# Attention and gated FFN on one core: q and k loaded in whole rows, outputs stored in 32-row pieces, masks taken off GpSimd

## The chip, the core and the metric

The kernel runs on one core of a Trainium2 chip. The metric is the device time of one execution, in microseconds (us). The kernel before took 558.26 us (median of three runs, 554.87 to 558.68). The profiled execution took 555.26 us, and its span from the first to the last recorded instruction is 553.5 us; times of single operations below are from that execution.

## The reference

Eight batches of eight heads, 576 positions, head size 64. Scores below the row's maximum less tau are cut, the rest goes through a softmax; the heads of a position make one row of 512, which is normalised by its root mean square and goes through a gated FFN with 1536 hidden values.

```python
scores = scale * np.matmul(q, k.transpose(0, 1, 3, 2))
thresh = np.max(scores, axis=-1, keepdims=True) - tau
scores = np.where(scores >= thresh, scores, -1000000000.0)
attn = softmax(scores)
x = np.matmul(attn, v)             # -> (4608, 512)
xn = x / rms(x) * rms_g
out = (silu(xn @ w_gate) * (xn @ w_val)) @ w_out
```

## The kernel before

**Tiles and stages.** The work is cut in 144 steps. One step takes a pair of heads and 128 query rows: 32 chunks of the first 512 positions of a batch ("m"), and 4 chunks that put the last 64 positions of two batches together ("v"), four head pairs each. A step goes through these operations:

- TensorE writes scores of both heads into PSUM (`s_ps`, L684).
- VectorE moves them to SBUF negated and scaled and takes the running minimum in the same instruction (`ssb`, `mx`, L717).
- GpSimd adds tau to that minimum (`nth`, L758).
- The threshold and the exponential. The list `WAYS` gives the way of a step from its number modulo 3, from step 16 (`FIRST`) on. The way "pp" is two activations on ScalarE that cut (L769) and one exponential of both heads (L776). The way "pg" does head 0 in that manner (L769, L773), and head 1 with an exponential on ScalarE (L788), a mask on GpSimd (L802) and their product on GpSimd (L807). Every third step is "pg", 42 in all.
- The fp16 weights `wsb` are transposed to `wt`, on TensorE for the first 16 steps (L821), and after that by a DMA transpose that SyncE issues (L836).
- TensorE multiplies by v for two steps at a time (AV, L854 and L859), and VectorE divides by the sum (L876, L878, L883).

After four steps a chunk is complete. It is squared (L900), scaled (L903 to L908) and transposed by DMA (`xnT`, L912). Groups of four chunks (the first two groups have two) go through the FFN: gate (L966), tanh (L980), value (L971), products on VectorE (L983, L988), output product (L1037, L1012 for the last group), eviction (L1050, L1052) and the store (L1058 for "m" chunks, L1062 for "v").

**Inputs.** Batches 0 and 1 come in natural rows and are transposed by TensorE. From batch 2 on (`BLOCKED`), `emit_block_loads` brings q and k so that VectorE can transpose them in blocks of 32 x 32 (L384, L389, L394). SBUF partition 64h + 32e + s gets, of the heads 4h to 4h + 3, half e of the head size, so a run in memory is 32 floats or 128 bytes. A batch takes eight such loads of 288 KB (L370). k is split as position = 18s + r, and q as position = 32r + s, so the 128 rows of an output chunk of these batches are consecutive rows, and one store writes them.

**Order.** Nothing of the order is left to the queues. Each operation is recorded with its engine, an assumed cost (`COST`, `DMA_NS`), a priority and its dependences; `order_ops` plays the program through with these costs, adds the offsets of `RANK` to the priorities, and writes out one fixed order for each engine. All loads, stores and DMA transposes are issued by SyncE in that one order, except for two late stores and one load on ScalarE and the output weights on GpSimd. [...] The second batch ahead is loaded while a batch is computed; a block load waits until the VectorE transposes of the block data before have read the buffer `qkx`.

Of the kernel before, what the change touches and what calls it, by code (L numbers as in the profile page):

```python
# [21 lines left out]
)  # L22
DMA_NS = dict(qkb=1900.0, qk=1250.0, tl=700.0, v=880.0, vt=350.0, wt=1700.0, xt=800.0, out=800.0, w=820.0, wo=2500.0)
SWITCH = 125.0

RANK = dict(
    ACT={"emit_ffn/ev": 260, "emit_ffn/store": 60, "emit_ffn/tanh": -350, "emit_k_tail/ev": -140, "emit_q_tail/ev": -100, "emit_qk/ev": 280,
        "emit_softmax/ex": 18, "emit_softmax/ex2": -350, "emit_softmax/prelu": 18, "emit_x/sq": -320},
    DVE={"emit_av/half": -10.4, "emit_blocks/turn_k": 30, "emit_blocks/turn_kt": 20, "emit_blocks/turn_q": 50, "emit_burst/ttr": -14.1, "emit_ffn/ev":
        140, "emit_ffn/gate": -80, "emit_ffn/silu": -13.4, "emit_k_tail/ev": -130, "emit_qk/ev": -100, "emit_softmax/ev": 410},  # L30
    PE={"emit_av/fn": -260, "emit_burst/fn": -160, "emit_ffn/gmm": 18.5, "emit_ffn/omm": 22, "emit_k_tail/tr": 250, "emit_q_tail/tr": -200,
        "emit_qk/tr": 170, "emit_softmax/tr": -190},
    POOL={"emit_softmax/mask": 110, "emit_softmax/nthr": -180, "emit_softmax/take": -170, "emit_x/mean": -60, "emit_x/norm": -41, "round_/<lambda>":
        -47.8, "main/<lambda>": 670, "main/cast": -260},
)
# [114 lines left out]
def kernel(  # L150
# [12 lines left out]
    nc = tc.nc  # L163
# [28 lines left out]
    LEAD = TAIL // 32  # L192
    qkx = sb("qkx", [128, 2 * S * NP])
    kx = qkx[:, 0:S * NP].rearrange("p (r a d) -> p r a d", a=NP, d=32)
    qx = qkx[:, S * NP:2 * S * NP].rearrange("p (a r d) -> p a r d", a=NP, d=32)
    qkn = [qkx[:, 1024 * i:1024 * (i + 1)].rearrange("p (j c h d) -> p j c h d", j=2, c=4, d=D) for i in range(NQK)]
# [159 lines left out]

    assert BLOCKED == 2 and S * NP < 1024 * NQK
    turned = []

    def emit_block_loads(b, prio):  # L360

        los = {}
        for j, src in ((1, k), (0, q)):
            before = turned[j] if turned else [x for t in tr_of for x in t[-NQK:]] + ([] if j else tail_load["use", 0])
            for h in range(2):
                for e in range(2):
                    def load(o, j=j, src=src, h=h, e=e):
                        rows = slice(64 * h + 32 * e, 64 * h + 32 * e + 32)
                        heads = src[b, NP * h:NP * h + NP, :, 32 * e:32 * e + 32]
                        nc.sync.dma_start(out=kx[rows] if j else qx[rows], in_=heads.rearrange("a (s r) d -> s r a d", r=RUN)  # L370
                                          if j else heads.rearrange("a (r s) d -> s a r d", r=RUN))

                    pr = prio + BLOCK_STEP * len([x for y in los.values() for x in y])
                    los.setdefault(j, []).append(gated(add("SP", COST["sp_qb"], pr, before, load, dma=DMA_NS["qkb"], bulk=True), pr))
                    los[j][-1].lat = LAT_QB
        turned[:] = [[], []]
        return los

    def emit_blocks(b, p, prio, los):
# [242 lines left out]
    def emit_batch_inputs(b):  # L622
# [318 lines left out]
    clock = [0.0]  # L941

    def emit_ffn(slot, parts, ready_step, pace, streamed):

# [80 lines left out]
        for j, (ci, _) in enumerate(parts):  # L1025
# [158 lines left out]
LAG = 8.0  # L1184
LAT_TR = 2000.0
LAT_LD = 2000.0
# [73 lines left out]
```

## Time and profile before

| what | value |
|---|---|
| span of the profiled execution | 553.5 us |
| TensorE busy | 527.7 us, 95% |
| VectorE busy | 467.7 us, 85% |
| ScalarE busy | 427.7 us, 77% |
| GpSimd busy | 255.9 us, 46% |
| DMA packets, bytes | 325,318, 89.03 MB |
| packets under 512 bytes | 307,840 |
| HBM read, written | 37.75 MB, 9.44 MB |
| last score product starts its burst | 490.2 us |

A matmul's end is modelled in the profile, so a TensorE that is called busy may still stand for part of that time. From some 50 us on, the attention of later chunks and the FFN of earlier ones share TensorE. After the last scores at 492 us there is only the FFN of the last groups left, in which TensorE is unbroken up to 548 us, and the last stores end at 553 us. The groups of instructions which the change touches are, in the page's columns (line, engine, operation, out and in, count, busy us, mean ns, idle time before them and its releaser):

```profile
L769 ACT ACTIVATE ssb<-ssb,nth 128x576 f32<-128x576 f32 x246 | 181.1, 765 | 35.5 <-POOL nth L758 35.2
L776 ACT ACTIVATE wsb<-ssb 128x1152 f16<-128x1152 f32 x102 | 118.2, 1159 | 3.4 <-DMA wt<-wsb 1.8
L802 POOL TENSOR_SCALAR wsb<-ssb,nth 128x576 f16<-128x576 f32 x42 | 72.5, 1726 | 37.6 <-DMA wt<-wsb 34.1
L807 POOL TENSOR_TENSOR wsb<-wsb,esb 128x576 f16<-128x576 f16 x42 | 53.7, 1279 | 4.0 <-ACT esb L788 0.7
L788 ACT ACTIVATE esb<-ssb,nth 128x576 f16<-128x576 f32 x42 | 32.3, 768 | 13.8 <-POOL nth L758 13.8
```

And the DMAs that it touches, in the list of DMA issues (out and in, queue, operation, count, KB each, median us from issue to landing):

```profile
out_dram<-osb SPq DMA_DIRECT2D x29, 256.0 KB, 2.9
qkx<-in_k_dram SPq DMA_DIRECT2D x24, 288.0 KB, 5.0
qkx<-in_q_dram SPq DMA_DIRECT2D x24, 288.0 KB, 5.2
wt<-wsb SPq DMA_TRANSPOSE x128, 3.9
```

### The profile page before, as it was taken

To read this page: it belongs to the slowest core of one execution; us is meant where nothing else is said; L and a number is where in the kernel's file an instruction comes from. 1 tells how busy PE (TensorE), PEld (TensorE's weight loads), DVE (VectorE), ACT (ScalarE), POOL (GpSimd) and SP (SyncE) were. 2 spreads that over 40 slices of the span, in tenths; PEclk is the share of its full clock that TensorE was granted. 3 is DMA by queue.
4 is the path that set the end of the run, shared out by engine and by line. 5 is a ranking of instruction groups with operands and counts; after the bars stand their busy time and mean duration, and the time that the engine had idled before them with its cause. 6 is when DMAs were issued, how large, how long until landed. Compare 5 with 4: busy or idle time off the path is not lost.

```text
span 553.5 us, 14260 instructions
## 1 busy us (share of the span) xinstructions
PE 527.7 (95%) x5336; PEld 276.9 (50%) x5336; DVE 467.7 (85%) x1342; ACT 427.7 (77%) x648; POOL 255.9 (46%) x418
## 2 busy tenths in 40 slices
PE   8999979997989999999999999999899999999996
PEld 4666646654545445544444545444454444445442
DVE  4898969986999899979998999899879997995661
ACT  5999978878888889778977898679857999893220
POOL 2378643384454654445455544365444653542000
PEclk9999999998999999999999999999989999999999
DMA  8999999999999899999999799999999767764102
GB/s 201 221 288 290 172 147 149 188 184 163 160 157 179 177 136 161 170 180 208 154 162 215 162 145 150 176 202 168 149 182 204 132 101 120 123 105 100 59 0 97
DMA packets 325318, 89.03 MB, mean 161 GB/s; under 512 B 307840, under 2 KB 317568, under 8 KB 325248
## 3 DMA queue, kind: packets, MB, share of 16 engines
q1 hardware_dynamic: 322320, 85.76, 90.1%
q0 software_dynamic: 1600, 1.57, 2.0%
q8 instruction: 42, 0.69, 0.6%
q10 hardware_dynamic: 1328, 0.79, 0.5%
q14 instruction: 28, 0.23, 0.2%
HBM read 37.75 MB, written 9.44 MB: 85 GB/s over the span
## 4 chain that ended last, share of the span: by engine, by line
PE 54%; DMA 18%; ACT 9%; DVE 8%; issue 5%; POOL 4%; SPq 1%; DVEq 0%; POOLq 0%; ACTq 0%
PE s_ps L684 16%; DMA wt<-wsb 11%; PE ring L966 10%; PE ring L971 10%; PE ring L1037 9%; DVE ssb L717 4%; ACT ssb L769 4%; PE ring L859 3%; ACT wsb L776 3%; DMA stg<-in_moe_w_val_dram 3%; DMA xnT<-xn 2%; PE s_ps L1012 2%; ACT th L980 1%; PE ring L854 1%; DVE sl L983 1%
## 5 line engine op out<-in xcount | busy, mean ns | idle before, releaser
L769 ACT ACTIVATE ssb<-ssb,nth 128x576 f32<-128x576 f32 x246 | 181.1, 765 | 35.5 <-POOL nth L758 35.2
L717 DVE CUSTOM_DVE_ANT_0 ssb<-s_ps,zrow 128x576 f32<-128x576 f32 (+8 forms) x288 | 171.5, 636 | 9.8 <-PE s_ps L684 7.6
L684 PE MATMUL s_ps<-qkt 64*64 64x288 f32 (+9 forms) x2240 | 173.8, 418 | 4.4 <-DVE mxp L717 3.4
L776 ACT ACTIVATE wsb<-ssb 128x1152 f16<-128x1152 f32 x102 | 118.2, 1159 | 3.4 <-DMA wt<-wsb 1.8
L684 PEld LDWEIGHTS s_ps<-qkt 64*64 64x64 f32 (+1 forms) x2240 | 82.6, 136 | 70.1 <-issue 28.7
L966 PE MATMUL ring<-xnT,wg 128*128 128x512 f16 (+1 forms) x464 | 109.7, 359 | 4.1 <-DMA xnT<-xn 4.1
L971 PE MATMUL ring<-xnT,wv 128*128 128x512 f16 (+1 forms) x464 | 109.8, 360 | 0.4 <-DVE hf L988 0.4
L758 POOL TENSOR_SCALAR nth<-mx 128x2 f32<-128x2 f32 x144 | 31.5, 219 | 149.4 <-DVE mx L717 140.9
L802 POOL TENSOR_SCALAR wsb<-ssb,nth 128x576 f16<-128x576 f32 x42 | 72.5, 1726 | 37.6 <-DMA wt<-wsb 34.1
L980 ACT ACTIVATE th<-ring 128x512 f32<-128x512 f32 (+1 forms) x116 | 62.8, 542 | 32.4 <-PE ring L966 32.1
L983 DVE SCALAR_TENSOR_TENSOR sl<-th,ring 128x512 f32<-128x512 f32 (+1 forms) x116 | 72.4, 626 | 13.6 <-ACT th L980 13.0
L966 PEld LDWEIGHTS <-wg 128*128 128x128 f16 x480 | 43.8, 98 | 53.6 <-issue 10.8
L971 PEld LDWEIGHTS <-wv 128*128 128x128 f16 x480 | 43.6, 98 | 53.9 <-issue 16.3
L717 DVE CUSTOM_DVE_ANT_0 ssb<-s_ps,zrow,mxp 128x128 f32<-128x128 f32 (+7 forms) x112 | 53.3, 512 | 20.0 <-PE s_ps L684 19.4
L807 POOL TENSOR_TENSOR wsb<-wsb,esb 128x576 f16<-128x576 f16 x42 | 53.7, 1279 | 4.0 <-ACT esb L788 0.7
L859 PE MATMUL ring<-va,wt 128*128 128x65 f16 (+1 forms) x1264 | 52.4, 194 | 0.0
L1037 PE MATMUL ring<-wo,hf 128*128 128x512 f16 x216 | 50.0, 381 | 0.0
L859 PEld LDWEIGHTS <-wt 128*128 128x128 f16 (+1 forms) x1280 | 47.2, 100 | 4.8
L788 ACT ACTIVATE esb<-ssb,nth 128x576 f16<-128x576 f32 x42 | 32.3, 768 | 13.8 <-POOL nth L758 13.8
L854 PE MATMUL ring<-va,wt 128*128 128x130 f16 (+1 forms) x158 | 32.0, 226 | 8.0 <-DMA wt<-wsb 7.8
L988 DVE TENSOR_TENSOR hf<-ring,sl 128x512 f16<-128x512 f32 (+1 forms) x59 | 37.1, 628 | 2.1 <-PE ring L971 0.3
L988 DVE TENSOR_TENSOR stg<-ring,sl 128x512 f16<-128x512 f32 (+1 forms) x57 | 35.7, 627 | 3.0 <-PE ring L971 0.4
(76 smaller groups left out, 494.9 us busy)
## 6 DMA issues: line engine op xcount, KB each, us to landing
vst<-in_v_dram SPq DMA_DIRECT2D x32, 256.0 KB, 4.3
out_dram<-osb SPq DMA_DIRECT2D x29, 256.0 KB, 2.9
qkx<-in_k_dram SPq DMA_DIRECT2D x24, 288.0 KB, 5.0
qkx<-in_q_dram SPq DMA_DIRECT2D x24, 288.0 KB, 5.2
stg<-in_moe_w_gate_dram SPq DMA_DIRECT2D x6, 512.0 KB, 5.8
stg<-in_moe_w_val_dram SPq DMA_DIRECT2D x6, 512.0 KB, 6.8
wt<-wsb SPq DMA_TRANSPOSE x128, 3.9
qkx<-in_k_dram SPq DMA_DIRECT2D x7, 256.0 KB, 5.2
```

The source lines that it names most:

```text
L684: nc.tensor.matmul(s_ps[h][rows, at:at + hi - lo], lhs(hs), k_of(bb, p, h)[hs, lo:hi], start=True, stop=True)
L717: nc.vector.tensor_tensor_reduce(out=ssb_of(s)[:, h, lo:hi], in0=s_ps[h][:, at:at + hi - lo], in1=zrow[:, lo:hi], scale=-1.0 / 8.0, scalar ...
L769: nc.scalar.activation(out=sb_[:, h], in_=sb_[:, h], func=PRELU, scale=-1.0, bias=nth[m][:, h:h + 1], **PRELU_KW)
L776: nc.scalar.activation(out=wsb[s % NW], in_=sb_, func=AF.Exp)
L802: nc.gpsimd.tensor_scalar(out=wsb[s % NW][:, h], in0=sb_[:, h], scalar1=nth[m][:, h:h + 1], scalar2=None, op0=ALU.is_le)
L859: nc.tensor.matmul(ring[o.slot[0]][rs, at:at + D + 1], w[:, 5 * h + j, rs], va[vi][:, p, 2 * j + h], start=False, stop=(h == 1 and j == 3))
L966: nc.tensor.matmul(ring[o.slot[0]][:, 0:n], wg[d][:, fs], xnT[slot][:, d, 0:n], start=(d == 0), stop=(d == 3))
L971: nc.tensor.matmul(ring[o.slot[0]][:, 0:n], wv[d][:, fs], xnT[slot][:, d, 0:n], start=(d == 0), stop=(d == 3))
L980: nc.scalar.activation(out=th[i][:, 0:n], in_=ring[g.slot[0]][:, 0:n], func=AF.Tanh, scale=0.5)
L983: nc.vector.scalar_tensor_tensor(out=sl[i][:, 0:n], in0=th[i][:, 0:n], scalar=1.0, in1=ring[g.slot[0]][:, 0:n], op0=ALU.add, op1=ALU.mult)
L988: nc.vector.tensor_tensor(out=hf[hi][:, 0:n], in0=ring[vv.slot[0]][:, 0:n], in1=sl[i][:, 0:n], op=ALU.mult)
L1037: nc.tensor.matmul(ring[(first or o).slot[0]], hf[hs[fc][0]][:, 128 * j:128 * (j + 1)], wo[:, fc], start=(fc == 0), stop=(fc == NFC - 1))
```

## The change

For batches 2 to 7, a block load now brings two heads in place of four, and of each position the whole row of 64 floats: 18 positions that follow each other, 4608 bytes, are one run. Both halves of the head size are wanted on different partitions (e = 0 and e = 1), so each head is loaded twice; the copy for e = 1 is put 32 floats earlier in its partitions, and after that the wanted half stands at the same address in all of them. The VectorE transposes then read 32 floats out of every 64. A batch has two groups of eight loads in place of one group of eight. The size of a load is 288 KB as before.

For this q has to be split as k is, position = 18s + r. So the rows of an output chunk are no longer consecutive: 32 rows with a distance of 18 belong together, and the store of such a chunk is made of four DMAs of 32 rows (`store_blocks`), that of the tail of a batch of two. For the late chunks of the last group, half of the pieces are issued by ScalarE.

`WAYS` has only "pp": GpSimd makes no masks, and ScalarE does both heads of every step. The assumed costs and the offsets of `RANK` are set anew, so the order of the instructions differs on every engine; the numbers of matmuls are the same. The new offsets are left out of the diff.

```diff
--- before.py
+++ after.py
@@ -20,18 +20,17 @@
     pool_tiny=302.0, pool_mean=944.0, pool_dma=880.0, cast_v=620.0, cast_vt=475.0, cast_w=665.0,
     sp=420.0, sp_v=600.0, sp_w=600.0, sp_tr=1300.0, sp_qk=680.0, sp_tl=630.0, sp_qb=600.0, turn=600.0, turn_t=210.0, turn_q=680.0,
 )
-DMA_NS = dict(qkb=1900.0, qk=1250.0, tl=700.0, v=880.0, vt=350.0, wt=1700.0, xt=800.0, out=800.0, w=820.0, wo=2500.0)
+DMA_NS = dict(qkb=750.0, qk=1250.0, tl=700.0, v=880.0, vt=350.0, wt=1700.0, xt=800.0, out=800.0, w=820.0, wo=2500.0)
 SWITCH = 125.0
 
 RANK = dict(
...
 )
 
 
@@ -190,9 +189,12 @@
     wo = sb("wo", [128, NFC, DM], FP16)
     RUN = S // 32
     LEAD = TAIL // 32
-    qkx = sb("qkx", [128, 2 * S * NP])
-    kx = qkx[:, 0:S * NP].rearrange("p (r a d) -> p r a d", a=NP, d=32)
-    qx = qkx[:, S * NP:2 * S * NP].rearrange("p (a r d) -> p a r d", a=NP, d=32)
+    GROUP = 2
+    WIDE = GROUP * RUN * D + 32
+    qkx = sb("qkx", [128, 2 * WIDE])
+    kx, qx = [qkx[:, WIDE * j + 32:WIDE * (j + 1)].rearrange("p (a r d) -> p a r d", a=GROUP, d=D)[:, :, :, 0:32] if 0 else
+              bass.AP(tensor=qkx.tensor, offset=qkx.offset + WIDE * j + 32, ap=[list(qkx.ap[0]), [RUN * D, GROUP], [D, RUN], [1, 32]])
+              for j in range(2)]
     qkn = [qkx[:, 1024 * i:1024 * (i + 1)].rearrange("p (j c h d) -> p j c h d", j=2, c=4, d=D) for i in range(NQK)]
     ktl, qtl = [[qkx[:, 1024 * NQK + at:1024 * NQK + at + H * D].rearrange("p (h d) -> p h d", d=D)] for at in (0, H * D)]
 
@@ -354,10 +356,10 @@
         for c in range(4):
             qk_ready[b, p, c] = done
 
-    assert BLOCKED == 2 and S * NP < 1024 * NQK
+    assert BLOCKED == 2 and WIDE < 1024 * NQK
     turned = []
 
-    def emit_block_loads(b, prio):
+    def emit_block_loads(b, g, prio):
 
         los = {}
         for j, src in ((1, k), (0, q)):
@@ -366,9 +368,10 @@
                 for e in range(2):
                     def load(o, j=j, src=src, h=h, e=e):
                         rows = slice(64 * h + 32 * e, 64 * h + 32 * e + 32)
-                        heads = src[b, NP * h:NP * h + NP, :, 32 * e:32 * e + 32]
-                        nc.sync.dma_start(out=kx[rows] if j else qx[rows], in_=heads.rearrange("a (s r) d -> s r a d", r=RUN)
-                                          if j else heads.rearrange("a (r s) d -> s a r d", r=RUN))
+                        at = WIDE * (1 - j) + 32 * (1 - e)
+                        a0 = NP * h + GROUP * g
+                        nc.sync.dma_start(out=qkx[rows, at:at + GROUP * RUN * D].rearrange("s (a n) -> s a n", a=GROUP),
+                                          in_=src[b, a0:a0 + GROUP].rearrange("a (s r) d -> s a (r d)", r=RUN))
 
                     pr = prio + BLOCK_STEP * len([x for y in los.values() for x in y])
                     los.setdefault(j, []).append(gated(add("SP", COST["sp_qb"], pr, before, load, dma=DMA_NS["qkb"], bulk=True), pr))
@@ -382,16 +385,16 @@
 
         def turn_k(o):
             nc.vector.transpose(out=dst[:, TAIL:S].rearrange("p (c k d) -> p c k d", c=4, d=32),
-                                in_=kx[:, LEAD:RUN, p].rearrange("p (k c) d -> p c k d", c=4))
+                                in_=kx[:, p % GROUP, LEAD:RUN].rearrange("p (k c) d -> p c k d", c=4))
 
         def turn_kt(o):
-            src = kx[:, 0:LEAD, p]
+            src = kx[:, p % GROUP, 0:LEAD]
             nc.vector.transpose(
                 out=dst[:, 0:2 * S].rearrange("p (j n) -> p j n", j=2)[:, :, 0:TAIL].rearrange("p j (t d) -> p j t d", d=32),
                 in_=bass.AP(tensor=src.tensor, offset=src.offset, ap=[list(src.ap[0]), [0, 2], list(src.ap[1]), list(src.ap[2])]))
 
         def turn_q(o):
-            nc.vector.transpose(out=dst[:, S + TAIL:2 * S + TAIL], in_=qx[:, p].rearrange("p r d -> p (r d)"))
+            nc.vector.transpose(out=dst[:, S + TAIL:2 * S + TAIL].rearrange("p (r d) -> p r d", d=32), in_=qx[:, p % GROUP])
 
         tk = gated(add("DVE", COST["turn"], prio, los[1] + free, turn_k), prio)
         tt = gated(add("DVE", COST["turn_t"], prio, los[1] + free, turn_kt), prio)
@@ -631,7 +634,7 @@
             for p in range(NP):
                 pr = base + 3.3 * p + 3
                 if b >= BLOCKED:
-                    los = emit_block_loads(b, pr - 3) if p == 0 else los
+                    los = los if p % GROUP else emit_block_loads(b, p // GROUP, pr - 3)
                     emit_blocks(b, p, pr, los)
                 else:
                     emit_qk(b, p, pr)
@@ -940,6 +943,11 @@
     count = dict(hf=0, gv=0, o=0, v=[])
     clock = [0.0]
 
+    def store_blocks(b, oi, n, row, at, late):
+        for i in range(n):
+            (nc.scalar if late and i % 2 else nc.sync).dma_start(
+                out=out[b * S:b * S + S].rearrange("(s r) d -> r s d", r=RUN)[row + i], in_=osb[oi][at + 32 * i:at + 32 * i + 32])
+
     def emit_ffn(slot, parts, ready_step, pace, streamed):
 
         n = 128 * len(parts)
@@ -1053,11 +1061,16 @@
 
             def store(o, oi=oi, kind=kind, b=b, c=c, late=late):
                 if kind == "m":
-                    rows = "(c n) d -> n c d" if b >= BLOCKED else "(n c) d -> n c d"
-                    dst = out[b * S:b * S + MAIN].rearrange(rows, c=4)[:, c]
+                    if b >= BLOCKED:
+                        store_blocks(b, oi, 4, 4 * c, 0, late)
+                        return
+                    dst = out[b * S:b * S + MAIN].rearrange("(n c) d -> n c d", c=4)[:, c]
                     (nc.scalar if late else nc.sync).dma_start(out=dst, in_=osb[oi])
                 else:
                     for e in range(2):
+                        if 2 * b >= BLOCKED:
+                            store_blocks(2 * b + e, oi, LEAD, MAIN // 32, 64 * e, False)
+                            continue
                         r0 = (2 * b + e) * S
                         nc.sync.dma_start(out=out[r0 + MAIN:r0 + S], in_=osb[oi][64 * e:64 * e + 64])
 
@@ -1065,7 +1078,7 @@
                     [last_out[j] if streamed else outs[-1], osb_use.get(oi)], ev,
                     frees=(mo, at))
             late = late and kind == "m"
-            osb_use[oi] = add("ACT" if late else "SP", COST["sp"] if kind == "m" else 1100.0, pr, [e], store,
+            osb_use[oi] = add("ACT" if late else "SP", (2200.0 if b >= BLOCKED else COST["sp"]) if kind == "m" else 2100.0 if 2 * b >= BLOCKED else 1100.0, pr, [e], store,
                               dma=DMA_NS['out'])
         if not streamed:
             for hi, _ in hs:
@@ -1182,7 +1195,7 @@
 PART_PRIO = 2.0
 SIZES = (2, 2, 4, 4, 4, 4, 4, 4, 4, 4)
 LAG = 8.0
-LAT_TR = 2000.0
+LAT_TR = 2500.0
 LAT_LD = 2000.0
 REL = (0.0, 0.0)
 REL_N = (0, 0)
@@ -1202,11 +1215,11 @@
 BACKLOG = 3500.0
 AV_PRIO = 2.5
 HALF_PRIO = 1.2
-WAYS = ("pg", "pp", "pp")
+WAYS = ("pp",)
 NSTAGE = 3
 NQK = 3
 BLOCKED = 2
-BLOCK_STEP = 1.4
+BLOCK_STEP = 0.6
 V_STEP = 1.0
 V_FROM = 6.0
 V_CAST = 9.0
```

More of the change, by code (lines that the diff above doesn't have):

```diff
@@ L22 @@
 )
-DMA_NS = dict(qkb=1900.0, qk=1250.0, tl=700.0, v=880.0, vt=350.0, wt=1700.0, xt=800.0, out=800.0, w=820.0, wo=2500.0)
+DMA_NS = dict(qkb=750.0, qk=1250.0, tl=700.0, v=880.0, vt=350.0, wt=1700.0, xt=800.0, out=800.0, w=820.0, wo=2500.0)
 SWITCH = 125.0
 RANK = dict(
[L27 to L34, printed above, removed]
+    ACT={"emit_ffn/ev": 300, "emit_ffn/store": 50, "emit_ffn/tanh": -293, "emit_k_tail/ev": -150, "emit_q_tail/ev": -130, "emit_qk/ev": 320,
+        "emit_softmax/ex2": -329.5, "emit_softmax/prelu": 80, "emit_x/sq": -310},
+    DVE={"emit_av/half": -20, "emit_blocks/turn_k": 30, "emit_blocks/turn_kt": 30, "emit_blocks/turn_q": 68, "emit_burst/ttr": -40, "emit_ffn/ev":
+        103, "emit_ffn/gate": -60, "emit_ffn/silu": -20, "emit_k_tail/ev": -120, "emit_qk/ev": -80, "emit_softmax/ev": 360},
+    PE={"emit_av/fn": -270, "emit_burst/fn": -140, "emit_ffn/gmm": 19, "emit_ffn/omm": 21, "emit_ffn/vmm": -110, "emit_k_tail/tr": 240,
+        "emit_q_tail/tr": -160, "emit_qk/tr": 90, "emit_softmax/tr": -120},
+    POOL={"emit_softmax/nthr": -90, "emit_x/mean": -80, "emit_x/norm": -20, "round_/<lambda>": -30, "main/<lambda>": 690, "main/cast": -220},
 )
```

## The prediction

> **What bounds the kernel now.** I read the page's slices first, then the waits of TensorE, then the issue queue of SyncE in the timeline, and last the landing times of the transposes.
>
> ```profile
> PE   8999979997989999999999999999899999999996
> DVE  4898969986999899979998999899879997995661
> ACT  5999978878888889778977898679857999893220
> DMA  8999999999999899999999799999999767764102
> q1 hardware_dynamic: 322320, 85.76, 90.1%
> PE 54%; DMA 18%; ACT 9%; DVE 8%; issue 5%; POOL 4%; SPq 1%; DVEq 0%; POOLq 0%; ACTq 0%
> ```
>
> TensorE is the engine with the least room (527.7 of 553.5 us), and the change gives it the same matrix products. So only time in which TensorE stands can be won. The DMA row is full up to slice 31 (about 430 us) and falls off after it: the last block loads of q and k are issued at 405 us. That stretch of 430 to 500 us is a free look at the attention loop without block loads, and I use it as the measure below.
>
> The waits of TensorE between 75 and 500 us:
>
> ```profile
> PE ring L854 <- DMA wt<-wsb: 7.8, 11, 1.8
> PE ring L966 <- DMA xnT<-xn: 4.1, 3, 3.5
> PE s_ps L684 <- DVE mxp L717: 3.4, 3, 2.6
> ```
>
> The wait that ends last in the steady part is that of the AV product (L854, L859) for a transposed weight tile. Ends of matmuls are modelled, so part of a stand counts as busy. From the starts of successive matmuls in the trace, less the spacing that each kind has when nothing holds it, the stands ahead of AV products are 14.7 us from 75 to 425 us (0.042 us per us) and 2.3 us from 425 to 500 us (0.030).
>
> Why are the tiles late? SyncE issues every transpose, load and store in one order. Its timeline, as start, length, operation:
>
> ```profile
> 191.39 0.67 SPq L370 DMA_DIRECT2D qkx<-in_k_dram  x1
> 192.79 5.74 SPq L836 DMA_TRANSPOSE wt<-wsb  x2
> 198.58 2.52 SPq L370 DMA_DIRECT2D qkx<-in_k_dram  x2
> 201.21 2.34 SPq L912 DMA_TRANSPOSE xnT<-xn  x1
> 203.66 1.40 SPq L836 DMA_TRANSPOSE wt<-wsb  x1
> 205.11 1.25 SPq L370 DMA_DIRECT2D qkx<-in_k_dram  x1
> 206.46 4.12 SPq L836 DMA_TRANSPOSE wt<-wsb  x2
> ```
>
> There is hardly a gap. An issue that follows a block load is long: two transposes take 5.74 us together, where one takes 1.29 us (median) from 430 to 500 us. The worst case is at 72.55 us: the issue of an xnT transpose takes 5.49 us right after a block load at 71.84 us, and TensorE's longest wait for xnT (3.5 us) is on that tile. The landing of the weight tiles says the same, from 75 to 425 us and then from 430 to 500 us:
>
> ```profile
> DMA to landing us min/median/max: 3.2/4.1/7.3
> DMA to landing us min/median/max: 3.2/3.3/5.5
> ```
>
> [...] The trace's packet records agree that short runs are dear: 128-byte packets take 16.2 ns each (8 bytes per ns), 2048-byte packets 101 ns (20 bytes per ns). [...] I give VectorE no gain from an idle GpSimd; L988 takes 0.69 us at 202.68 us beside a mask and 0.69 us at 207.54 us without one.
>
> **The change part by part.**
>
> Block loads. Before: 48 DMAs of 288 KB in 128-byte packets, 110,592 packets x 16.2 ns / 16 engines = 112 us of all DMA engines, 2.3 us for each load. After: 96 DMAs, 64 runs of 4608 bytes each; at the 20 bytes per ns of the 2048-byte packets a run is an estimated 228 ns, a load 0.91 us, all of them 87 us. HBM reads 14 MB more, but the engines are freed of 25 us of 512, and no transpose stands behind more than about 0.9 us of load in place of 2.3. On SyncE the 48 issues sum to 44 us in the trace; 96 at 0.4 (the issue of a 128-row store) to 0.6 us (the usual one of a block load) are 38 to 58 us. The transposes behind them averaged 1.87 us over 103 of them up to 420 us, against 1.34 us after it: up to 0.53 x 103 = 55 us of SyncE come free, and 0.3 x 25 = 8 us on xnT.
>
> Stores. Batches from 2 on store each chunk in four pieces; the tails twice as many. The built order has 475 rows on SyncE in place of 351: 48 loads and 76 stores more. At 0.40 us (median of L1058) that is 30 us. In sum SyncE gets 63 us back and spends 30, and between -6 and +14 on the loads. A chunk now holds the queue some 1.6 us in a row; queued behind it are the next weight transposes, for which AV waits. The planner puts them where it expects slack, with 2.2 us of cost for four.
>
> Masks. 42 pairs of L802 and L807 leave GpSimd (72.5 + 53.7 = 126 us). In their 42 steps ScalarE does two L769 and a double L776 (2 x 765 + 1159 = 2689 ns) in place of 765 + 680 + 768 = 2213 ns: 0.476 x 42 = 20 us more, on an engine at 77%. Hidden by TensorE's own work: ScalarE was busy 24.3 of 25 us from 425 to 450 us while TensorE stood for 0.7 us ahead of AV. What comes back is latency: ScalarE waited 35.2 + 13.8 = 49 us for the small thresholds of L758, some of them queued behind masks of 1.7 us. Bounds for what of this TensorE sees: 0 (all of it hidden) and 4 us (a twelfth); I take 2.
>
> Strided transposes on VectorE (L384, L389, L394), one more wait of loads for transposes per batch (qkx now holds two head pairs per half of a batch): same element counts, 0; the second group's loads are hidden by the three steps that a pair of heads lasts ahead.
>
> Order. After the last score product the changed order keeps 296 FFN matmuls of 512 columns in place of 252: 44 x 0.216 = 9.5 us moved behind. TensorE is unbroken there (from 494 to 548 us), so this moves work and is worth nothing by itself; it says that the plan counts on reaching the last score 9.5 us earlier.
>
> End. The last stores in pieces: a few more issues of 0.34 us, smaller landings: 0.5 us loss.
>
> Sum. AV stands at the quiet rate: (0.042 - 0.030) x 350 = 4.2 us. The xnT wait at 80 us: 3.5 us. Latency of the thresholds: 2 us. End: -0.5 us. Together 9.2 us: 558.3 - 9.2 = 549.1, say 549 us. The 3.4 us of score waits stay.
>
> **The rivals.**
> (1) No change that can be measured: the pieces of stores and doubled loads give SyncE back what the short runs took, and AV waits as before. For: 30 us of stores at worst meet 14 us more of loads, near the 63 us freed; stands in the quiet stretch are not gone. Against: the long issues come behind block loads alone. Only the xnT wait is won, less the end: 558.3 - 3 = 555.
> (2) Slower: a block of four stores delays a transpose just when AV needs it, and ScalarE with 20 us more sits on the path in a third of the 42 steps (6.7 us). If a quarter of 27 chunks cost 1.6 us (10.8 us) and the other gains of 9.2 us hold: 558.3 + 10.8 + 6.7 - 9.2 = 566.6, say 566. For: three engines are near 9 tenths all along. Against: SyncE has slack once issues are short, as after 430 us.
> (3) More than forecast: nearly all stands ahead of AV go (14.7 us), the xnT wait too (4.1 us), with 2 us of latency: 558.3 - 20 = 538.
>
> **How the numbers follow.** Forecast 0.55, (3) 0.1, (1) 0.22, (2) 0.13. The range reaches from the full removal, 538, to between (1) and (2), 560. Faster by over 1% (below 552.7): the forecast and (3), 0.65. Within 1%: 0.22. Slower: 0.13.
>
> **What would show it.** Right: the issue of a weight transpose falls to a mean near 1.4 us, its landing to about 3.4 us median; packets fall by 104,000 and the DMA share below 90%; TensorE's waits for wt and xnT fall from 12 to about 5 us; GpSimd loses 126 us and ScalarE gains 20. Wrong: SyncE without gaps again with stores in the place of long issues, landings still at 4 us, or ScalarE as the releaser of AV's tiles. A run of 4608 bytes that takes far more than 228 ns would break the first step.

## The result, and the profile after

The changed kernel takes **577.66 us** (median of four runs, 575.34 to 580.83), beside 556.57 us (553.97 to 558.68) for the kernel before on the same chip. The ratio is 1.0385, with a 95% interval of 1.0309 to 1.0461: slower by some 21 us, where 549 us and a gain were forecast; it is above the forecast's range of 538 to 560 us. Ratios here and below are of runs in the fast state alone; the one slow run, 564.17 us in experiment 4, stands in its range of times but not in its ratio.

The page of the changed kernel (span 573.6 us): busy tenths in 40 slices, the main DMA queue (packets, MB, share of the 16 DMA engines' span), and the chain of work that ended last, by engine and by line.

```profile
PE   8998999886999998989998989988989999999994
...
DMA  8999999999799999999999999998999885761103
q1 hardware_dynamic: 219984, 100.18, 91.9%
PE 41%; DMA 26%; ACT 17%; DVE 6%; issue 5%; POOL 3%; SPq 0%; ACTq 0%; DVEq 0%; POOLq 0%
```

Packets fell by 102,000, as they were meant to. (The trace records each DMA packet with its size and duration; each run of the q and k loads is one packet in these two kernels. Engine time below is the sum of such durations over 16 engines.) The time that they take did not: 0.901 x 553.5 = 499 us of the 16 engines before, 0.919 x 573.6 = 527 us after. The forecast had it at 25 us less; it is 28 us more. The q and k loads are 12 of these 28 (112 to 124 us); the rest comes from all other packets; those of 256 bytes, most of them the transposes', took 303 us in place of 297. The DMA row now stays full into slice 32. TensorE's row has 8, 8 and 6 in slices 8 to 10 and an 8 in seven later ones, where it was at 9 nearly throughout. On the chain of work TensorE's share falls from 54% to 41%, DMA rises from 18% to 26%, and ScalarE from 9% to 17%.

What TensorE waited for between 75 and 500 us (total us, times, longest):

```profile
PE ring L857 <- DMA wt<-wsb: 20.5, 21, 2.7
PE ring L974 <- DMA xnT<-xn: 4.7, 3, 2.7
PE s_ps L687 <- DVE mxp L720: 3.8, 3, 2.7
```

The wait that was to shrink, that of the AV product (now L857) for a transposed weight tile, grew from 7.8 to 20.5 us; the other two stayed. Measured as in the prediction, from the starts of matmuls, the stands ahead of AV products from 75 to 490 us went from some 17 to some 31 us. How the undisturbed spacing is taken moves both by a few us, and the growth of 14 us hardly.

All engines in the stretch with block loads and in the one after it; the columns are the window, its length, then busy us and number of instructions of TensorE, of its weight loads, of VectorE, ScalarE and GpSimd, then TensorE's granted clock, DMA share and GB/s. First the kernel before, then after:

```profile
75.00:425.00 350.00, 334.96 (x3482) 170.76 (x3479) 312.47 (x923) 282.93 (x424) 173.61 (x273) 0.99 1.07 171
425.00:500.00 75.00, 74.49 (x794) 36.73 (x793) 67.27 (x203) 69.07 (x104) 40.14 (x61) 1.00 0.71 119
```

```profile
75.00:425.00 350.00, 321.92 (x3391) 163.24 (x3388) 304.24 (x904) 293.76 (x422) 72.64 (x201) 0.99 1.08 201
425.00:500.00 75.00, 72.72 (x795) 35.69 (x793) 64.88 (x201) 68.18 (x96) 16.03 (x45) 1.00 0.88 146
```

In the same 350 us TensorE does 13 us less work. The DMA engines have hardly any time left in either kernel (shares just over 1, so packets overlap in the records): the bytes went from 171 to 201 GB/s, yet nothing came free.

The landing of the weight tiles, in the two stretches of the prediction (75 to 425 us, then 430 to 500 us), kernel after:

```profile
DMA to landing us min/median/max: 3.2/4.9/9.0
DMA to landing us min/median/max: 3.2/3.5/5.0
```

Where block loads run, a tile lands at 4.9 us in place of 4.1, not at 3.4 as the forecast had it; where none run, it is 3.5. SyncE's timeline after (start, length, operation) shows the long issues still there:

```profile
207.48 1.52 SPq L373 DMA_DIRECT2D qkx<-in_q_dram  x3
209.11 6.55 SPq L839 DMA_TRANSPOSE wt<-wsb  x2
```

Two transposes behind three block loads take 6.55 us to issue, longer than the 5.74 us of the example before. The mean issue of a weight transpose up to 420 us is 1.94 us (1.87 before; 1.4 forecast).

What the masks' removal did, in the groups (count, busy us and mean ns, idle us before them and its releaser), and after them the DMA issues (count, KB each, median us to landing):

```profile
L772 ACT ACTIVATE ssb<-ssb,nth 128x576 f32<-128x576 f32 x288 | 209.6, 765 | 23.4 <-POOL nth L761 22.9
L779 ACT ACTIVATE wsb<-ssb 128x1152 f16<-128x1152 f32 x144 | 166.8, 1159 | 30.6 <-DMA wt<-wsb 28.8
```

```profile
qkx<-in_k_dram SPq DMA_DIRECT2D x48, 288.0 KB, 5.3
...
out_dram<-osb SPq DMA_DIRECT2D x98, 64.0 KB, 1.8
...
wt<-wsb SPq DMA_TRANSPOSE x128, 4.6
```

ScalarE's wait for thresholds fell from 35.2 + 13.8 to 22.9 us. But the exponential L779 now idles 28.8 us for a transpose to release its weight buffer (1.8 us before, when the 34.1 us of this kind stood at GpSimd's mask). So late transposes meet ScalarE as well as TensorE.

The time can be split at the last score product. It ended at 492.2 us before and 499.7 after; the FFN work of TensorE behind it took 56.4 and 65.9 us; the end behind TensorE 4.9 and 8.0 us. So 20.1 us of span are 7.5 us of attention, although 9.5 us of FFN work had left it, 9.5 us of FFN tail, and 3.1 us of end. The end, on SyncE's timeline of the kernel after:

```profile
552.45 13.10 SPq L948 DMA_DIRECT2D out_dram<-osb  x12
566.24 3.71 SPq L948 DMA_DIRECT2D out_dram<-ssb  x6
570.05 0.84 SPq L948 DMA_DIRECT2D out_dram<-osb  x2
```

The last pieces of 32 rows are issued one by one, down to 570.9 us; the kernel before issued its last store in 0.34 us.

### The profile page after: what moved, and what is told of

The parts are those of the page before. It is cut to its first block, busy times and chain, and to the rows that moved or that the text cites. A ratio compares the mean times of both kernels' runs of the same rounds, so it can differ in the third digit from the quotient of the medians.

```text
span 573.6 us, 14361 instructions
## 1 busy us (share of the span) xinstructions
PE 529.8 (92%) x5336; PEld 276.2 (48%) x5336; DVE 468.0 (82%) x1342; ACT 445.2 (78%) x648; POOL 129.5 (23%) x334
## 3 DMA queue, kind: packets, MB, share of 16 engines
q1 hardware_dynamic: 219984, 100.18, 91.9%
HBM read 51.91 MB, written 9.44 MB: 107 GB/s over the span
## 4 chain that ended last, share of the span: by engine, by line
PE 41%; DMA 26%; ACT 17%; DVE 6%; issue 5%; POOL 3%; SPq 0%; ACTq 0%; DVEq 0%; POOLq 0%
DMA wt<-wsb 21%; PE s_ps L687 11%; ACT ssb L772 8%; PE ring L1045 8%; PE ring L974 7%; PE ring L979 6%; ACT wsb L779 6%; DVE ssb L720 4%; DMA xnT<-xn 2%; PE ring L862 2%; ACT th L988 2%; DMA stg<-in_moe_w_val_dram 2%; PE s_ps L1020 2%; PE ring L857 1%; PE s_ps L979 1%
## 5 line engine op out<-in xcount | busy, mean ns | idle before, releaser
L772 ACT ACTIVATE ssb<-ssb,nth 128x576 f32<-128x576 f32 x288 | 209.6, 765 | 23.4 <-POOL nth L761 22.9
L779 ACT ACTIVATE wsb<-ssb 128x1152 f16<-128x1152 f32 x144 | 166.8, 1159 | 30.6 <-DMA wt<-wsb 28.8
L687 PE MATMUL s_ps<-qkt 64*64 64x288 f32 (+9 forms) x2240 | 171.9, 415 | 5.0 <-DVE mxp L720 3.8
L687 PEld LDWEIGHTS s_ps<-qkt 64*64 64x64 f32 (+1 forms) x2240 | 80.9, 135 | 70.6 <-issue 27.6
L979 PE MATMUL ring<-xnT,wv 128*128 128x512 f16 (+1 forms) x456 | 107.9, 359 | 0.3 <-DVE hf L996 0.3
L988 ACT ACTIVATE th<-ring 128x512 f32<-128x512 f32 (+1 forms) x116 | 62.8, 542 | 44.2 <-PE ring L974 44.0
L991 DVE SCALAR_TENSOR_TENSOR sl<-th,ring 128x512 f32<-128x512 f32 (+1 forms) x116 | 71.9, 624 | 17.8 <-ACT th L988 17.7
L857 PE MATMUL ring<-va,wt 128*128 128x130 f16 (+1 forms) x160 | 32.5, 227 | 20.5 <-DMA wt<-wsb 20.5
L862 PEld LDWEIGHTS <-wt 128*128 128x128 f16 (+1 forms) x1280 | 47.1, 100 | 4.3
L1045 PE MATMUL ring<-wo,hf 128*128 128x512 f16 x204 | 47.9, 379 | 0.0
L1045 PE MATMUL ring<-wo,stg 128*128 128x512 f16 x156 | 38.5, 392 | 0.0
L996 DVE TENSOR_TENSOR stg<-ring,sl 128x512 f16<-128x512 f32 (+1 forms) x57 | 35.5, 625 | 2.3
L996 DVE TENSOR_TENSOR hf<-ring,sl 128x512 f16<-128x512 f32 (+1 forms) x57 | 35.3, 623 | 2.1 <-PE ring L979 0.4
L857 PEld LDWEIGHTS <-wt 128*128 128x128 f16 (+1 forms) x160 | 14.2, 99 | 40.1 <-DMA wt<-wsb 23.7
L1045 PEld LDWEIGHTS <-hf 128*128 128x128 f16 x216 | 20.1, 98 | 24.6 <-issue 2.5
```

Of the source, the lines that this page charges most:

```text
L687: nc.tensor.matmul(s_ps[h][rows, at:at + hi - lo], lhs(hs), k_of(bb, p, h)[hs, lo:hi], start=True, stop=True)
L772: nc.scalar.activation(out=sb_[:, h], in_=sb_[:, h], func=PRELU, scale=-1.0, bias=nth[m][:, h:h + 1], **PRELU_KW)
L779: nc.scalar.activation(out=wsb[s % NW], in_=sb_, func=AF.Exp)
L857: nc.tensor.matmul(ring[o.slot[0]][rs, at:at + 2 * (D + 1)], w[:, 4, rs], va[vi][:, p, 8:10].rearrange("p e d -> p (e d)"), start=True, st ...
L862: nc.tensor.matmul(ring[o.slot[0]][rs, at:at + D + 1], w[:, 5 * h + j, rs], va[vi][:, p, 2 * j + h], start=False, stop=(h == 1 and j == 3))
L979: nc.tensor.matmul(ring[o.slot[0]][:, 0:n], wv[d][:, fs], xnT[slot][:, d, 0:n], start=(d == 0), stop=(d == 3))
```

## The experiments

Two theories fit this profile. **D, the DMA engines:** the whole-row loads need more DMA-engine time, not less, and the transposes share those engines (their packets go through the same main queue). The packet records say that a run of 4608 bytes takes 322 ns: 6144 x 322 / 16 = 124 us, against 112 us for the short runs. **S, the stores:** 104 pieces in place of whole stores hold SyncE's queue, and the transposes stand behind them. A third, **A**, that ScalarE with both heads of every step sets the pace, was a part of the prediction's second rival.

### 1. Whole-row loads cut to half a run (from the kernel after)

```diff
-    out=qkx[rows, ...].rearrange("s (a n) -> s a n", a=GROUP),
-    in_=src[b, a0:a0 + GROUP].rearrange("a (s r) d -> s a (r d)", r=RUN))
+    out=...[:, :, 0:RUN * D // 2],
+    in_=...[:, :, 0:RUN * D // 2])
```

> The changed kernel, with each run of the block loads cut to 2304 bytes: half of every row group of q and k isn't loaded, and its place holds older data; the order of instructions is that of the changed kernel. Theory D (the DMA engines: doubled q and k cost them 124 us where the short runs cost 112, and the weight transposes queue behind): landing of the weight tiles from 75 to 425 us falls from 4.9 to about 4.0 us median, TensorE's waits for them from 20.5 to under 10 us, time 577.7 to about 562 us (the late FFN work and the longer end stay). Theories S (store pieces on SyncE) and A (ScalarE without the masks' help): within 4 us of 577.7.

VectorE also clears the buffer once at the start, here and in experiment 12 (not in the lines shown).

543.07 us (541.79 to 545.69), ratio to the kernel before 0.9776 (0.9732 to 0.9820). The 2304-byte runs took 149 ns, 57 us in all. TensorE's waits from 75 to 500 us, and the landing of the tiles from 75 to 425 us:

```profile
PE s_ps L688 <- DVE mxp L721: 3.4, 3, 2.7
PE ring L858 <- DMA wt<-wsb: 1.3, 3, 0.6
PE ring L975 <- DMA xnT<-xn: 0.3, 1, 0.3
```

```profile
DMA to landing us min/median/max: 3.2/3.8/6.6
```

With as many loads, issues and store pieces, in the same order, the waits for both kinds of transposed tiles all but go. So theory D holds: 66 us less of DMA-engine time are worth a ratio of 0.9776 / 1.0385, some 34 us. It leaves open whether bytes of memory or time of the engines count; experiment 10 tells these apart.

### 2. One store for each chunk (from the kernel after)

```diff
-        for i in range(n):
-            (nc.scalar if late and i % 2 else nc.sync).dma_start(out=..., in_=osb[oi][at + 32 * i:at + 32 * i + 32])
+        r0 = b * S + 32 * row
+        (nc.scalar if late else nc.sync).dma_start(out=out[r0:r0 + 32 * n], in_=osb[oi][at:at + 32 * n])
```

> The changed kernel, with one store for each chunk and each tail in place of four and two: rows of the output come out in another order; the order of all other instructions is that of the changed kernel. Theory S (the 76 more stores hold SyncE, 0.43 us each, and transposes start late): waits for weight tiles fall from 20.5 to about 8 us, time to about 562 us. Theory D: only the longer end of 3 us goes, plus up to 2 us: 572 to 575 us.

565.88 us (562.44 to 567.61), ratio 1.0173 (1.0123 to 1.0222). The pieces cost 1.0385 / 1.0173, 2.1% or some 12 us, so theory S holds too, for a part. Of it 3.3 us are the end behind TensorE (8.0 to 4.7 us); the last score product ends 6.5 us earlier, at 493.2 us. AV still waits, in TensorE's list of waits:

```profile
PE ring L857 <- DMA wt<-wsb: 16.7, 18, 2.7
```

### 3 and 4. The masks, put back and taken off

The kernel after with masks again (`WAYS = ("pg", "pp", "pp")`, with offsets for the two operations in `RANK`), and the kernel before without them:

```diff
-WAYS = ("pg", "pp", "pp")
+WAYS = ("pp",)
```

> The changed kernel, with masks on GpSimd again in every third step from step 16, with the mask offsets of the kernel before. Theory A (ScalarE's 17 us more delay the weights): time about 562 us. Theories D and S: ScalarE had room, 574 to 581 us.

> The kernel before, with only the masks taken off GpSimd; all loads, stores, costs and offsets as before. Theory A: 566 us or more against 556.6. Theories D and S: 552 to 561 us.

With masks back: 575.87 us (573.87 to 577.0), ratio 1.0356 (1.0316 to 1.0396), not told apart from the 1.0385 of the change. Taken off the kernel before: 554.08 us (552.08 to 564.17), ratio 0.9981 (0.9952 to 1.0010). ScalarE works 427.2 and 444.1 us in the two, GpSimd 256.8 and 128.8 us. The 17 us more of ScalarE cost nothing that can be measured, and theory A falls. ScalarE's 17% of the chain are no sign of it either: with the same work and order, but cheaper loads (experiment 10), its share is 9%. The DMA queue's packets took 93.3% of 550.1 us in the latter, 513 us against 499 in the kernel before, and nothing was lost. So the sum over all packets is a loose measure, and 28 us more of it are no loss by themselves; the time of one run of the loads is the firmer one (314 to 326 ns in the four kernels with these loads). The 2 us of latency that the prediction took as a gain lie within both intervals: neither shown nor excluded.

### 5. Transfers alone, first attempt

A kernel of transfers only: loads of both kinds, then stores whole and in pieces, with a VectorE pass over the tile between the kinds of loads.

> No attention and no FFN: only transfers, issued by SyncE, in phases that a VectorE pass over the buffer keeps apart; the output holds zeros. Phases: (1) 8 loads in the old manner (128-byte runs, 288 KB each), (2) 8 in the new manner (4608-byte runs on 32 partitions), (3) 4 loads of 4608-byte runs on 128 partitions (576 KB each), (4) 8 loads of 2048-byte runs on 32 partitions (256 KB), (5) 8 of 2048-byte runs on 128 partitions, (6) 16 stores of 128 rows, (7) 16 chunks stored in four pieces of 32 rows with a distance of 18. If a run is dear because of its 32 partitions, packets of (2) take about 320 ns and of (3) under 240, and (4) differs from (5) in the same way. If it is the length, (2) and (3) both take about 320. If it is the traffic of the whole kernel, (2) and (3) both take about 230 ns.

118.57 us. The stores did not wait for the loads, so the times of whole phases can't be read from it. The packet records can: a 4608-byte run takes some 320 ns (median) when a load goes to 32 partitions, and 178 ns when it goes to 128. They settle one more thing. The loads of the change read every byte from HBM twice, once for each half (51.91 MB read in the whole kernel, 37.75 before), and that could be what makes their runs slow. In the fourth phase every byte is read once. Its 2048-byte runs follow each other in memory and went as packets of 8192 bytes, 585 ns each (mean) on 32 partitions: 14 bytes per ns, hardly other than 4608 bytes in 315 ns (mean). So neither the second reading nor the length of a run is the cause. Experiment 9 repeats it with the phases apart.

### 6. Store pieces in the kernel before

```diff
+                    if b >= BLOCKED:
+                        for i in range(4):
+                            (nc.scalar if late and i % 2 else nc.sync).dma_start(
+                                out=dst[32 * i:32 * i + 32], in_=osb[oi][32 * i:32 * i + 32])
+                        return
```

> The kernel before, with stores of batches 2 to 7 in four pieces of 32 rows (tails in two), rows and assumed costs as before. If the pieces cost the same here as in the changed kernel (11.8 us by the second experiment, 3.3 of them at the end): 565 to 569 us. If they hurt only where the DMA engines are overfull with doubled loads: 558 to 562 us, the end and little else.

The tails are split in two in the same manner (not in the lines shown).

566.88 us (564.67 to 567.68), ratio 1.0235 (1.0182 to 1.0289): the pieces alone cost the kernel before 13 us. TensorE's wait for the tiles:

```profile
PE ring L854 <- DMA wt<-wsb: 18.0, 18, 2.3
```

It rises from 7.8 to 18.0 us while the landing keeps its median of 4.1 us. So the pieces make the transposes late in the queue, before their issue; the loads of the change make them late behind their issue (landing 4.9 us in place of 4.1).

### 7. The new order on the kernel before

`WAYS`, the offsets of `RANK` and `LAT_TR` of the kernel after, on the loads and stores of the kernel before.

```diff
-LAT_TR = 2000.0
+LAT_TR = 2500.0
-WAYS = ("pg", "pp", "pp")
+WAYS = ("pp",)
```

> The kernel before, with loads and stores as they were, but with the new order's offsets, its assumed latency of a transpose, and no masks on GpSimd. Theory P (the new order is a bad one by itself; 44 FFN matmuls left for the end): 562 us or more. Theory D: with short-run loads and whole stores this order gives 550 to 558 us, as fast as the kernel before.

556.59 us (553.44 to 561.1), ratio 1.0059 (1.0032 to 1.0085). The offsets, off the loads and stores they were set for, cost 3 us (the masks' removal included). Taking factors: 1.0385 = 1.0208 (pieces) x 1.0059 (order) x 1.0113, and the last, some 6 us, is left for the loads; the intervals of the two runs alone make it uncertain by about 3 us. That they multiply is assumed, and no run did the loads alone.

### 8. A plan that knows what the loads cost (from the kernel after)

The order is planned with `qkb` = 750 for the movement of a block load. A load of 64 runs of 322 ns on 16 engines takes 1290.

```diff
-DMA_NS = dict(qkb=750.0, ...)
+DMA_NS = dict(qkb=1300.0, ...)
```

> The changed kernel, with the plan told that a block load takes the DMA engines 1300 ns, about what its packets took (4 x 322 ns), in place of 750; the same transfers in another order. Theory P: a plan with the right cost wins most of the loss back, under 565 us. Theory D: the bytes stay, 573 to 582 us.

571.74 us (568.6 to 573.97), ratio 1.0325 (1.0271 to 1.0379), which overlaps that of the change. In part the wait moves:

```profile
PE s_ps L687 <- DVE mxp L720: 13.5, 12, 3.1
PE ring L857 <- DMA wt<-wsb: 1.1, 2, 0.9
```

Tiles are no longer late for AV (20.5 to 1.1 us), and scores wait for the VectorE pass instead (3.8 to 13.5 us). But the waits of the list also fall in sum, from 30 to 16 us, and the share of DMA in the chain from 26% to 7%. TensorE's mean granted clock was lower in these runs, 0.969 to 0.981 against 0.982 to 0.991 for the change. If its 534 us of work stretched with it, that is some 6 us (an estimate from these figures). So this plan did not win most of the loss back; what a better plan is worth at an equal clock stays open.

### 9. Transfers with their phases apart

The kernel of transfers again, a VectorE pass over the whole tile between all phases: eight loads of 288 KB in 128-byte runs (L30), eight in 4608-byte runs on 32 partitions each (L35), four of 576 KB in 4608-byte runs on 128 partitions (L40), eight of 288 KB in 2304-byte runs on 128 partitions (L43), those of L35 issued by SyncE and ScalarE in turn, 16 stores of 256 KB (L46), 64 of 64 KB (L50). It ran once.

> As the fifth experiment, which ran stores beside loads, but each phase waits for the one before it: 8 loads in the old manner, 8 in the new manner, 4 of 4608-byte runs on 128 partitions, 8 of 2304-byte runs on 128 partitions, 8 in the new manner issued by SyncE and ScalarE in turn, 16 whole stores, the same rows in 64 pieces of 32 rows; no attention and no FFN, and the output holds parts of q and k. If 32 partitions are what makes a run dear: 4608-byte packets near 320 ns on 32 partitions and near 180 ns on 128, 2304-byte ones on 128 near 95 ns, [...]. If not: the same rate in all phases of long runs.

Its timeline (start, length, engine, line, operation; for the VectorE lines, the idle time before and its releaser):

```profile
9.42 13.30 SPq L30 DMA_DIRECT2D t<-in_k_dram  x8
25.75 4.43 DVE L26 TENSOR_SCALAR t<-t 128x8192 f32<-128x8192 f32 x1 [16.36 <-DMA t<-in_k_dram]
30.21 3.84 SPq L35 DMA_DIRECT2D t<-in_k_dram  x8
42.25 4.43 DVE L26 TENSOR_SCALAR t<-t 128x8192 f32<-128x8192 f32 x1 [12.07 <-DMA t<-in_k_dram]
46.71 1.79 SPq L40 DMA_DIRECT2D t<-in_q_dram  x4
55.58 4.43 DVE L26 TENSOR_SCALAR t<-t 128x8192 f32<-128x8192 f32 x1 [8.90 <-DMA t<-in_q_dram]
60.03 3.91 SPq L43 DMA_DIRECT2D t<-in_q_dram  x8
69.94 4.43 DVE L26 TENSOR_SCALAR t<-t 128x8192 f32<-128x8192 f32 x1 [9.94 <-DMA t<-in_q_dram]
...
90.42 10.00 SPq L46 DMA_DIRECT2D out_dram<-t  x16
103.14 4.43 DVE L26 TENSOR_SCALAR t<-t 128x8192 f32<-128x8192 f32 x1 [12.75 <-DMA out_dram<-t]
107.59 30.31 SPq L50 DMA_DIRECT2D out_dram<-t  x64
139.56 4.43 DVE L26 TENSOR_SCALAR t<-t 128x8192 f32<-128x8192 f32 x1 [32.00 <-DMA out_dram<-t]
```

The VectorE pass starts when a phase has landed. The first three phases move the same 2.36 MB, from first issue to landing in 16.3, 12.0 and 8.9 us. So whole rows take 12.0 / 16.3 = 0.74 of the time of short runs for each byte, and the change moves twice the bytes: 2 x 0.74 = 1.47. The fourth phase, again 2.36 MB but in 2304-byte runs on 128 partitions, takes 9.9 us: shorter runs are no gain in themselves. In the packet records a 128-byte run takes 13.0 ns here, a 4608-byte run 307 ns on 32 partitions and 196 ns on 128 (means). For the loads of the kernel that is 110,592 x 13.0 / 16 = 90 us against 6144 x 307 / 16 = 118 us, 1.31; in the full kernels it is 112 and 124 us, since the short runs lose more there (16.2 ns) than the long ones (322 ns). Two issuing queues make hardly a difference (11.6 us in place of 12.0).

The stores: 4.19 MB in 12.7 us whole and in 32.0 us in pieces. The pieces are held by their issue, 30.31 / 64 = 0.47 us each, one after the other on SyncE.

### 10. The same loads on all partitions (from the kernel after)

As many loads of as many bytes, each as 128 runs of 2304 bytes on 128 partitions in place of 64 runs of 4608 on 32. The values of q and k come to wrong places, so the scores are other ones.

```diff
-    out=qkx[rows, at:at + GROUP * RUN * D].rearrange("s (a n) -> s a n", a=GROUP),
-    in_=src[b, a0:a0 + GROUP].rearrange("a (s r) d -> s a (r d)", r=RUN))
+    at = WIDE * (1 - j) + 32 + 576 * (2 * h + e)
+    out=qkx[:, at:at + 576],
+    in_=src[b, a0:a0 + GROUP].rearrange("a (p n) d -> (a p) (n d)", n=9))
```

> The changed kernel with block loads of the same number and bytes, each to all 128 partitions (128 runs of 2304 bytes), so that q and k stand in wrong places; order and stores as in the changed kernel. If the loss comes from the time that loads hold the DMA engines (theory D, by the 32 partitions): loads take some 73 us of the engines in place of 124, and the time falls to about 552 us, most of the way to the 543.1 of halved runs. If it comes from the bytes read from HBM: within 5 us of 577.7.

551.17 us (547.38 to 554.28) beside 551.81 us for the kernel before on this chip; ratio 0.9985 (0.9961 to 1.0009). The runs took 120 ns each, 92 us in all in place of 124. Its wait for weight tiles from 75 to 500 us, its landing from 75 to 425 us, and its main DMA queue from the page:

```profile
PE ring L858 <- DMA wt<-wsb: 8.1, 9, 2.1
```

```profile
DMA to landing us min/median/max: 3.2/4.2/7.2
```

```profile
q1 hardware_dynamic: 226128, 100.18, 87.9%
```

With the 100.18 MB of the change to the byte, with its store pieces and its order, 0.9985 / 1.0385 = 0.9615 or some 22 us come back. So it is not the 14 MB more that count, nor the number of loads: it is the time that the runs hold the DMA engines, and in experiments 5 and 9 this differs with how many partitions a load goes to (320 against 178 ns, median, and 307 against 196 ns, mean, for a 4608-byte run on 32 and on 128). The landing and the AV wait return to those of the kernel before (4.1 and 7.8 us).

### 11. Less DMA time, more TensorE work (the kernel before, no masks)

```diff
-N_ALT = 16
+N_ALT = 48
```

`WAYS` is that of experiment 4. 16 more weight tiles are transposed by TensorE in place of a DMA.

> The kernel before without masks on GpSimd, and every second of the steps 17 to 47 with its weights transposed by TensorE (16 fewer DMA transposes, 2.3 us of the DMA engines each). Theory D says that the kernel before is held by the DMA engines too: 37 us less of their time should win 5 to 12 us, 543 to 549. If TensorE is the bound: 16 x 0.5 us more work, 558 to 562.

564.23 us (562.42 to 565.97), ratio 1.0200 (1.0135 to 1.0265): slower. The main DMA queue falls to 84.5% of its span, TensorE rises to 535.0 us and VectorE to 478.1. A miss for theory D as I had stretched it: here less DMA time did not pay for the work that it put on TensorE and VectorE. Which of the two it is, or the order made anew, this run does not tell apart.

### 12. Half of the loads in the kernel before

Two of the four heads of each block load are left out; order, stores and masks as before.

```diff
-    out=kx[rows] if j else qx[rows], in_=heads.rearrange(...)
+    # k: qkx[rows, 0:RUN * 64] <- heads[0:2]      q: qx[rows][:, 0:2] <- heads[0:2]
```

> The kernel before, in the same order of instructions, with two of the four heads left out of every block load of q and k (the other halves of the buffer keep older data, so its scores are not those of the reference). The 128-byte packets fall from 110,592 to 55,296, worth 56 us of the 16 DMA engines. Theory D taken further (the kernel before is itself held by the DMA engines): 545 us or less. If the DMA engines only began to bound with the change, and the kernel before has enough room: 550 to 556 us.

536.72 us (536.5 to 538.28), ratio 0.9691 (0.9633 to 0.9749). TensorE's waits from 75 to 500 us, and its page's chain:

```profile
PE s_ps L688 <- DVE mxp L721: 3.5, 2, 2.6
PE ring L970 <- DMA xnT<-xn: 0.5, 1, 0.5
```

```profile
PE 80%; ACT 6%; DVE 5%; issue 3%; DMA 3%; POOL 2%; SPq 1%; DVEq 0%; POOLq 0%
```

The wait for weight tiles is gone from the list, TensorE is 80% of the chain, and the mean issue of a weight transpose falls to 1.50 us. So the kernel before was itself held by its block loads. Their own issue on SyncE is also 14 us shorter (44 to 30 us), which this run does not tell apart from the DMA engines; in experiment 10 it is no shorter than in the change (55 us against 52), and the time fell nevertheless. A change that really freed the engines would have paid; a ratio of 0.9691 is what 112 - 47 = 65 us of engine time, with that issue, are worth there.

Of the kernels that do the whole computation, none is measurably below the kernel before; the nearest is the kernel before without masks (0.9981).

## Why the prediction was wrong

**What bounds the kernel** was read rightly: only stands of TensorE could be won, AV's wait for weight tiles ended last, and block loads are what makes the tiles late. Experiment 12 shows it, with more to win (17 us) than the 4.2 us that the forecast gave to AV.

**Block loads: the step that failed.** The prediction took "20 bytes per ns of the 2048-byte packets", 228 ns for a run and 87 us for all. The runs took 322 ns and 124 us, so the engines got 12 us more work where 25 us less were booked: a term mis-sized by 37 us, and with its sign turned. The rate was borrowed from transfers that span 128 partitions, and the new loads go to 32. In the trace a load takes 1.29 us where the forecast had 0.91. Experiment 9 shows the difference (307 ns on 32 partitions against 196 on 128 for the same 4608 bytes), and experiment 10 what it is worth in the kernel (92 us in place of 124 for the same bytes). Why the number of partitions counts, no run here shows.

**SyncE's issue time** failed with it. The prediction booked up to 63 us back, from transposes that no longer stand behind 2304 runs. Their mean issue went from 1.87 to 1.94 us: a 36th of the runs in each load did not shorten it. (The difference itself says little: with these same loads it is 1.77 to 2.02 us in experiments 2, 3 and 8.) It fell to 1.64 us in experiment 10, with the 96 loads of the change and twice its runs in each, but 92 us of the DMA engines in place of 124, and to 1.50 us in experiment 12, whose loads take 47 us. So in these runs it fell with the time that the loads hold the engines; by what means, no run shows.

**Stores: the second failure.** The number of issues and their price were about right (104 pieces, 48 us in all; forecast: 76 more issues at 0.40 us). Taken as hidden by SyncE's slack, they were not: 12 us in the change, 13 us in the kernel before. The end lost 3.1 us, not 0.5, because the last eight pieces on SyncE go out one by one behind the last product, from 566.2 to 570.9 us. This is the first half of the second rival, which gave it 10.8 us; that this is so near is in part luck, since it did not count the end. Its second half, ScalarE in the way, did not occur (experiments 3 and 4). The rival's 566 us fell short because it still counted the gains of the loads.

**Masks** came out as worked: GpSimd 126 us less, ScalarE 17.5 us more (20 forecast), hidden. That VectorE gains nothing from an idle GpSimd was the author's estimate; VectorE was busy 467.7 us before and 468.0 after, and its products on PSUM took 626 and 628 ns in the mean before (L983, L988 into `hf`), 624 and 623 after (L991, L996). Its transposes, for which the prediction put 0, took 42.0 us in place of 40.8.

**Order.** The 9.5 us of FFN work behind the last scores are in the trace as forecast (65.9 against 56.4 us). "Worth nothing by itself" held only if the last score came 9.5 us earlier; it came 7.5 us later. The order was planned with 750 ns for a load that takes 1290. In experiment 10, the same order with loads of 92 us in all, the last score product ends at 475.7 us, 16.5 us earlier than in the kernel before.

**The sum.** Against the kernel before: some 12 us of store pieces, 3 us of order, and about 6 us of loads by the factors of experiment 7, in place of 9.2 us won. Against the forecast, experiment 10 gives the shares more directly. Its loads take 92 us of the engines, near the 87 that the forecast counted on, and its ratio is 0.9985, where the forecast is 549.1 / 558.3 = 0.984. So of the 5.5% between forecast and result the load term is 4.0%, some 22 us. The other 1.5%, some 8 us, would have been missed even with the loads priced nearly right. The store pieces, which experiment 10 keeps, are the likeliest cause; no run took them away from it. The sign that the prediction named for being wrong, a run that takes far more than 228 ns with landings still at 4 us, is what the trace shows.

## What to carry to other kernels

Price a DMA in engine time, runs x ns of a run / 16, and take the ns from a transfer with the same span of partitions; bytes per run alone did not tell it here (307 and 196 ns for 4608 bytes on 32 and on 128 partitions). When a longer run is bought with doubled bytes, its rate has to more than double; here it went from 7.9 to 14.3 bytes per ns (128 / 16.2 and 4608 / 322), 1.8 times. Where one queue issues both stores and the transposes that a product waits for, do not take small stores as hidden: here 76 more issues, some 30 us of that queue, cost 12 to 13 us, about 3 of them at the end of the changed kernel, where nothing hides them.

## What was not expected of the hardware

- The same 4608-byte run takes 307 ns where loads go to 32 partitions each and 196 ns where they go to 128; 2304-byte runs on 128 partitions take 120 ns in the kernel, so half the run length gave three quarters of the time for the same bytes (92 us against 124).
- The issue time of a DMA transpose fell with the load of the DMA engines: a mean of 1.77 to 2.02 us in four kernels whose q and k loads take 120 to 125 us of them, and of 1.64 us where as many loads of as many bytes, in twice as many runs, took 92 us.
- Stores of 64 KB from one queue were held by their issue (0.47 us each, 30.3 us in sum): 4.19 MB took 32.0 us in 64 pieces and 12.7 us in 16.
